# One attention unit's query path moves from plain projections with TensorE transpositions to split projections with VectorE transpositions, under a new order of the program

## The chip, the cores and the metric

The kernel runs on one core of a Trainium2 chip. Its time is the device time of one execution in microseconds (us). Five engines work side by side, each through its own queue in program order: TensorE (PE, with its weight loads as PEld), VectorE (DVE), ScalarE (ACT), GpSimd (POOL) and SyncE (SP), which issues all the transfers. An instruction starts when its engine is free and the semaphores that it waits on have come.

## The reference: what is computed

A linear attention over 8 batches of 8 heads (576 tokens, 64 wide, 128 random features), whose output is the input of one feed-forward block with a softmax gate and a layer norm over 4608 tokens.

```python
def phi(x):
    proj = np.einsum('bhsd,df->bhsf', x, w_phi)
    proj = proj - np.max(np.abs(proj), axis=-1, keepdims=True)
    return np.concatenate([np.exp(proj), np.exp(-proj)], axis=-1)
q_p, k_p = (phi(q), phi(k))
kv = np.einsum('bhsf,bhsd->bhfd', k_p, v)
num = np.einsum('bhsf,bhfd->bhsd', q_p, kv)      # den: the same with z, the sum of k_p
...
h = x @ w_in                                      # x: num / den, 4608 x 512
e = np.exp(h - h_max); sm = e / e.sum(); solu = h * sm
ln = (solu - mu) / np.sqrt(var + 1e-06) * g_ln
out = ln @ w_out
```

## The kernel before, in words

The attention is cut into 16 units (two per batch, four heads each), and a unit into two halves of two heads ("sub" 0 and 1). A unit's keys are projected in three groups of token tiles (4, 1 and 4 tiles: `k_rows`, line 557, and `by_block`, line 551, into PSUM tiles `pjk`); VectorE takes the row maximum (`m<-pjk`) and subtracts it (`ek<-pjk,m`); ScalarE makes the two exponentials. `visit` (line 594) then sums keys times values on TensorE (`kv`), 80 records of the trace, and from the fifth half on it first runs the previous half's queries against their finished sums (`num`, 72 records).

The queries have two paths, chosen by the tuple `Q_PLAIN` (line 30).

The **plain** path (units in `Q_PLAIN`; lines 612 to 651) goes as the keys do: float32 projections with tokens on the partitions (`pjq`), a maximum (`m<-pjq`) and a subtraction (`dq<-pjq,m`) on VectorE per group and head, then 24 transpositions on TensorE (`dT<-ident,dq`), and ScalarE's exponentials straight out of PSUM (`fq<-dT`).

The **split** path (all other units; lines 653 to 710) splits the queries into a high part (ScalarE, `hq`) and a remainder (GpSimd, `lq`), and projects them in three products with features on the partitions (`pq`). The maximum lies across partitions there. So VectorE transposes blocks of 32 by 32 (`blk<-pq`), reduces (`m<-blk`) and combines the quarters in seven small instructions (the rest of `q_max`, line 681); GpSimd subtracts (`blk<-blk,m`, `q_sub`, line 696); VectorE transposes back (`fq<-blk`, `q_back`, line 702); ScalarE makes the exponentials from SBUF (`fq<-fq`).

The feed-forward block runs in 18 groups of two token tiles. A group's input comes back through HBM (`xT<-dx`), GpSimd and ScalarE make sums and high and low parts (`S`, `ah`, `al`), and TensorE forms seven products of six matmuls each (`U` four times, `h` three times: `product`, line 978). VectorE joins them in PSUM (`moe_keep`, line 993; `moe_join`, line 1012, a custom instruction `h<-h,c` or `h<-U,c`). Softmax, layer norm, a turn of the tile through HBM and 24 matmuls `o` per tile follow. The first product can't start before the input weights are prepared: eight loads of 64 bit numbers (`wraw`) are made into float32 by two VectorE instructions each, `w<-wraw` (`w_low_bits`, line 394) and `w<-whi,w` or `w<-wraw,w` (`w_join_bits`, line 400), and split on ScalarE and GpSimd (`wb_l`, `wt_l`; four of the eight make the output weights, which are needed at the first `o`).

All of this is a list of some 2600 operations (`plan.op`). Nothing is scheduled when the kernel is built: `SEQUENCE` (lines 55 to 192) is the whole program order as a list of operation numbers, and `Plan.order` (line 243) only walks it and hands each tile its buffer. Each engine's queue is this list with the other engines left out. PSUM has six one-bank tiles for everything (`PSUM_BUFS`, line 45), handed out in the list's order. Every instruction has line 274 in the trace, the helper that keeps program order, so it is found by its tiles.

```python
Q_PLAIN = (0, 1, 2)
...
for u in range(2 * B):
    b, qd = u // 2, u % 2
    qsp = u not in Q_PLAIN
```

Of the kernel before, what the change touches and what calls it, by code (L numbers as in the profile page):

```python
# [29 lines left out]
Q_PLAIN = (0, 1, 2)  # L30
# [255 lines left out]
def linear_attention_then_moe(ctx: ExitStack, tc, qT, qT2, kT, v, w_phi, w_in, g_ln, w_out, out):  # L286
# [490 lines left out]
    def features(n):  # L777
        u, sub = n // 2, n % 2
        return [(u, "qe", sub, c, *x) for c in range(2) for x in (((0,), (1,)) if u not in Q_PLAIN else QP)]

    QP = [(j, s) for j in range(2) for s in range(2)]
# [3 lines that stand above are left out]
        st = states[u] = {"u": u, "b": b, "qd": qd}  # L785
# [532 lines left out]
```

## Time and profile before

| | us |
|---|---|
| median of 3 runs | 640.41 (637.32 to 641.12) |
| the profiled execution | 634.97 |
| its span, first to last instruction | 633.2 |
| PE busy in the span | 617.8 |
| DVE, ACT, POOL busy | 475.3, 458.1, 432.0 |

The profiled execution is the one that the trace shows; it lies below the three runs. Its span is 1.77 us shorter than its time. Times within the trace count from the span's first instruction. PE's busy share counts overlapping matmuls once, and a matmul that is stretched by a late operand still counts as busy.

### The profile page before, as it was taken

The numbers are of one execution on the slowest core, as the hardware profiler recorded it, in microseconds if no ns is written. First come the engines' busy times: TensorE is split into PE (matmuls) and PEld (weight loads), VectorE is DVE, ScalarE is ACT, GpSimd is POOL, SyncE is SP. The second block draws the span as 40 slices with busy tenths as digits, with TensorE's granted clock in tenths as the row PEclk, the third lists the DMA queues.
The fourth block names the chain that finished last, engine by engine and source line by source line (L and its number), as shares of the span: only waits on it lengthen the run. The fifth ranks groups of instructions, "written<-read, shape, count | busy, mean of one in ns | idle before, by whom it ended". The sixth has DMA issues, their size and how long they took to land.

```text
span 633.2 us, 19010 instructions
## 1 busy us (share of the span) xinstructions
PE 617.8 (98%) x7558; PEld 525.0 (83%) x7558; DVE 475.3 (75%) x995; ACT 458.1 (72%) x842; POOL 432.0 (68%) x468
## 2 busy tenths in 40 slices
PE   6999899999999999999999999999999999999997
PEld 5988688878888888888888888888888888888887
DVE  6999999787868885877876779988897973453540
ACT  4999798677957877477877667887776686466743
POOL 0568998777658864856786586657876675487732
PEclk9999999999999999999999999999999999999999
DMA  8886354754438374455574627545535355356441
GB/s 282 310 274 206 95 162 165 217 144 158 133 115 228 118 218 146 132 143 129 155 229 158 166 87 227 161 126 194 157 128 145 103 165 182 82 158 182 150 134 67
DMA packets 100200, 103.38 MB, mean 163 GB/s; under 512 B 50448, under 2 KB 73232, under 8 KB 99600
## 3 DMA queue, kind: packets, MB, share of 16 engines
q1 hardware_dynamic: 100112, 102.18, 52.8%
q8 instruction: 59, 0.97, 0.6%
q14 instruction: 29, 0.24, 0.1%
HBM read 64.92 MB, written 37.22 MB: 161 GB/s over the span
## 4 chain that ended last, share of the span: by engine, by line
PE 88%; DVE 6%; ACT 2%; DMA 2%; issue 1%; SPq 0%; ACTq 0%; DVEq 0%
PE o L274 31%; PE U L274 15%; PE h L274 12%; PE num L274 10%; PE kv L274 9%; PE pjk L274 5%; PE pq L274 4%; DVE m L274 2%; DVE w L274 1%; DVE ek L274 1%; PE pjq L274 1%; DVE dq L274 1%; DMA xT<-dx 1%; ACT fq L274 1%; DMA out<-os 1%
## 5 line engine op out<-in xcount | busy, mean ns | idle before, releaser
L274 PE MATMUL o<-w_out_h,uhs 128*128 128x512 f32 x280 | 112.4, 402 | 0.0
L274 POOL TENSOR_TENSOR uls<-uTs,uhs 128x1024 fp32r<-128x1024 f32 x35 | 83.7, 2390 | 41.9 <-ACT uhs L274 28.9
L274 PE MATMUL o<-w_out_l,uhs 128*128 128x512 f32 x280 | 109.4, 391 | 0.0
L274 PE MATMUL o<-w_out_h,uls 128*128 128x512 f32 x280 | 109.2, 390 | 0.0
L274 ACT ACTIVATE ek<-ek 128x512 f32<-128x512 f32 (+1 forms) x160 | 90.6, 584 | 16.9 <-DVE ek L274 16.1
L274 PEld LDWEIGHTS num<-kvf,fq 128*64 128x64 f32 x2304 | 70.0, 138 | 9.6 <-issue 5.0
L274 PE MATMUL kv<-rv,ek 128*64 128x65 f32 x2048 | 76.9, 222 | 0.0
L274 PE MATMUL num<-kvf,fq 128*64 128x65 f32 x2304 | 74.4, 223 | 0.1
L274 POOL TENSOR_TENSOR blk<-blk,m 128x1152 f32<-128x1152 f32 x26 | 55.6, 2138 | 27.3 <-DVE m L274 27.3
L274 ACT ACTIVATE fq<-fq 128x640 f32<-128x640 f32 (+1 forms) x104 | 69.4, 679 | 6.1 <-DVE fq L274 5.6
L274 PEld LDWEIGHTS kv<-rv,ek 128*64 128x64 f32 x2048 | 71.0, 138 | 0.8 <-ACT fq L274 0.2
L274 ACT ACTIVATE eu<-h,nm 128x1024 f32<-128x1024 f32 x36 | 40.1, 1115 | 36.4 <-DVE nm L274 31.7
L274 PEld LDWEIGHTS o<-w_out_h,uhs 128*128 128x128 f32 x280 | 52.6, 188 | 12.5 <-issue 0.2
L274 POOL TENSOR_TENSOR al<-S,ah 128x512 fp32r<-128x512 f32 x36 | 47.5, 1320 | 21.8 <-ACT ah L274 20.9
L274 PEld LDWEIGHTS o<-w_out_h,uls 128*128 128x128 f32 x280 | 52.6, 188 | 11.2
L274 PEld LDWEIGHTS o<-w_out_l,uhs 128*128 128x128 f32 x280 | 52.6, 188 | 10.3
L274 POOL TENSOR_TENSOR y<-E,rc 128x512 f32<-128x512 f32 x64 | 43.6, 704 | 21.3 <-DVE rc L274 19.1
L274 DVE TENSOR_REDUCE m<-pjk 128x4 f32<-128x512 f32 (+1 forms) x80 | 48.9, 620 | 11.4 <-PE pjk L274 11.1
L274 DVE SCALAR_TENSOR_TENSOR eu<-h,eu 128x1024 f32<-128x1024 f32 x36 | 43.8, 1218 | 18.1 <-ACT eu L274 17.7
L274 DVE STREAM_TRANSPOSE ub<-eu 128x1024 f32<-128x1024 f32 x35 | 43.1, 1233 | 14.3 <-ACT eu L274 5.5
L274 DVE STREAM_TRANSPOSE blk<-pq 128x320 f32<-128x320 f32 (+1 forms) x104 | 43.4, 455 | 10.8 <-PE pq L274 10.7
L274 POOL TENSOR_TENSOR lq<-rawq,hq 128x576 fp32r<-128x576 f32 x26 | 37.2, 1432 | 20.9 <-ACT hq L274 20.1
(113 smaller groups left out, 1558.4 us busy)
## 6 DMA issues: line engine op xcount, KB each, us to landing
du<-ub SPq DMA_DIRECT2D x35, 512.0 KB, 3.0
uTs<-du SPq DMA_DIRECT2D x140, 128.0 KB, 3.2
dx<-y SPq DMA_DIRECT2D x32, 288.0 KB, 2.7
out<-os SPq DMA_DIRECT2D x35, 256.0 KB, 3.0
rv<-in_v SPq DMA_DIRECT2D x32, 264.0 KB, 4.1
rawk<-in_k SPq DMA_DIRECT2D x32, 256.0 KB, 4.0
xT<-dx SPq DMA_DIRECT2D x64, 128.0 KB, 3.3
rawq<-in_q SPq DMA_DIRECT2D x26, 288.0 KB, 3.9
```

The lines of the kernel that those rows point to most:

```text
L274: return self.tc.keep_in_program_order(method(*args, **kwargs))
```

## The change

Unit 2 (the first unit of batch 1) leaves `Q_PLAIN`, so that its queries take the split path, as those of units 3 to 15 do. The operations are numbered anew, and `SEQUENCE` is another list: not the old one with unit 2's rows replaced, but one whose first rows already differ (keys ahead of queries at the start). No function changes.

```diff
-Q_PLAIN = (0, 1, 2)
+Q_PLAIN = (0, 1)
...
 SEQUENCE = (
-    120, 3, 121, 4, 76, 110, 124, 87, 177, 78, 20, 95, 0, 122, 88, 200, 77, 125, 96, 111, 79, 89, 83, 80, 81,
...
+    76, 3, 4, 78, 79, 83, 80, 110, 111, 81, 0, 112, 87, 84, 85, 90, 120, 113, 86, 91, 116, 117, 126, 114, 77,
...
```

Two places show what the list does. The first is VectorE's queue in the stretch in which unit 2's queries are handled, between the turn of unit 1's output (`y<-y`) and the last weight pieces. Before, with `m<-pjq` and `dq<-pjq,m` as unit 2's maximum and subtraction and `blk<-pq` as a transposition of unit 3:

```order
L274 TENSOR_TENSOR ek<-pjk,m 128x4x128
L274 TENSOR_REDUCE m<-pjq 128x2
L274 TENSOR_TENSOR dq<-pjq,m 128x256
L274 TENSOR_REDUCE m<-pjk 128x4 x2
L274 TENSOR_TENSOR ek<-pjk,m 128x4x128
L274 STREAM_TRANSPOSE blk<-pq 128x320 x2
L274 TENSOR_REDUCE m<-pjq 128x4
L274 TENSOR_TENSOR dq<-pjq,m 128x512
L274 TENSOR_REDUCE m<-pjq 128x4
L274 TENSOR_TENSOR dq<-pjq,m 128x512
L274 TENSOR_SCALAR w_5_1255<-wraw_909 128x1024
L274 TENSOR_SCALAR w_7_1257<-wraw_1054 128x1024
```

After the change the same stretch holds unit 2's transpositions, reduction and the small instructions that combine quarters (`m_1067` is unit 2's maximum, first half):

```order
L274 TENSOR_TENSOR ek<-pjk,m 128x4x128
L274 STREAM_TRANSPOSE blk<-pq 128x320 x2
L274 RECIPROCAL rc<-rc 128x18
L274 STREAM_TRANSPOSE blk<-pq 128x256 x2
L274 TENSOR_REDUCE m_1067<-blk 128x36
L274 COPY m4p<-m_1067 64x36
L274 TENSOR_TENSOR m_1067<-m_1067,m4p 64x36
L274 COPY m4p<-m_1067 32x36
L274 TENSOR_TENSOR m_1067<-m_1067,m4p 32x36 x4
L274 STREAM_TRANSPOSE y<-y 128x576
L274 TENSOR_REDUCE m<-pjk 128x4
L274 STREAM_TRANSPOSE blk<-pq 128x320 x2
```

So VectorE has more instructions of other kinds here, and the remaining weight pieces move behind them. The second place is TensorE's queue from unit 2's first visit to its second. Before, with unit 2's transpositions (`dT`) and plain projections (`pjq`) around a part of unit 3's split projection (`pq`):

```order
L274 MATMUL kv<-vz_70,ek 64x65 x2
L274 MATMUL dT<-ident,dq 128x128 x6
L274 MATMUL pjq<-wph,rawq_1038 128x256
L274 MATMUL pjk<-wph,rawk 128x128 x8
L274 MATMUL dT<-ident,dq 128x128 x6
L274 MATMUL pq<-hq,w_hh 128x320 x2
L274 MATMUL pq<-hq,w_ll 128x320 x2
L274 MATMUL pq<-lq,w_hh 128x320 x2
L274 MATMUL pjq<-wph,rawq_1019 128x128 x8
L274 MATMUL num<-kvf,fq 64x65 x36
```

After, from the same last rows of the visit on, with unit 2's split projections ahead of and behind a key projection:

```order
L274 MATMUL kv<-vz_70,ek 64x65 x2
L274 MATMUL pq<-hq,w_hh 128x320 x2
L274 MATMUL pq<-hq,w_ll 128x320 x2
L274 MATMUL pq<-lq,w_hh 128x320 x2
L274 MATMUL pq<-hq,w_hh 128x256 x2
L274 MATMUL pq<-hq,w_ll 128x256 x2
L274 MATMUL pq<-lq,w_hh 128x256 x2
L274 MATMUL pjk<-wph,rawk 128x128 x8
L274 MATMUL pq<-hq,w_hh 128x320 x2
L274 MATMUL pq<-hq,w_ll 128x320 x2
L274 MATMUL pq<-lq,w_hh 128x320 x2
L274 MATMUL pq<-hq,w_hh 128x256 x2
```

The transpositions `dT` of unit 2, which before stood between and behind the first feed-forward products too, are gone from TensorE's queue, and with them changes between float32 and split (fp32r) matmuls. From the last of the first group's seven products on (`h` with the weights `wt_h`, six matmuls) both queues hold the same set of matmuls.

## Rows read from the trace of the kernel before

**Rows 1.** The page's line on the busy time of each engine (share of the span, number of instructions).

```profile
PE 617.8 (98%) x7558; PEld 525.0 (83%) x7558; DVE 475.3 (75%) x995; ACT 458.1 (72%) x842; POOL 432.0 (68%) x468
```

**Rows 2.** Busy time by stretch: the stretch in us, its length, busy us and number of instructions of PE, PEld, DVE, ACT and POOL, granted clock, DMA share, GB/s.

```profile
5.96:68.40 62.44, 56.18 (x1125) 49.11 (x1125) 59.27 (x93) 53.11 (x116) 39.34 (x28) 1.00 0.79 267
...
83.38:629.99 546.61, 544.51 (x6211) 461.43 (x6208) 402.40 (x877) 390.06 (x697) 376.50 (x421) 1.00 0.52 155
629.99:633.20 3.21, 0.00 (x0) 0.00 (x0) 0.00 (x0) 0.47 (x1) 0.00 (x0) 1.00 0.12 41
```

**Rows 3.** What VectorE waited for between 5.96 and 83.38 us: instruction, who released it, us in total, times, longest. Of the first row's 7.0 us, 5.96 lie ahead of VectorE's first instruction.

```profile
DVE m L274 <- PE pjq L274: 7.0, 3, 6.0
DVE m L274 <- PE pjk L274: 1.0, 3, 0.5
DVE h L274 <- PE h L274: 0.6, 1, 0.6
...
DVE rc L274 <- ACT rc L274: 0.3, 1, 0.3
DVE y L274 <- POOL y L274: 0.2, 1, 0.2
```

**Rows 4.** TensorE in order of time: start, us, instruction, merged count. The first product `U`, and the last product of the first group, which stands right behind unit 3's first visit.

```profile
68.40 0.47 PE L274 MATMUL U<-wb_h,ah 128*128 128x512 f32 x1 [2.15 <-DVE blk L274]
...
83.38 0.50 PE L274 MATMUL h<-wt_h,ah 128*128 128x512 f32 x1
```

**Rows 5.** VectorE in order of time, the same columns: a pair of short transpositions, a combination of quarters from its reduction to its successor, the joining instruction that the last product waits for, and the transposition back of one half with its successor.

```profile
67.81 0.77 DVE L274 STREAM_TRANSPOSE blk<-pq 128x256 f32<-128x256 f32 x2
...
72.41 1.34 DVE L274 TENSOR_REDUCE m<-blk 128x36 f32<-128x1152 f32 x1
...
75.17 0.67 DVE L274 TENSOR_TENSOR c<-U,c 128x512 f32<-128x512 f32 x1
...
81.48 0.70 DVE L274 CUSTOM_DVE_ANT_0 h<-U,c 128x512 f32<-128x512 f32 x1
...
85.82 1.55 DVE L274 STREAM_TRANSPOSE fq<-blk 128x320 f32<-128x320 f32 x4
87.29 1.22 DVE L274 SCALAR_TENSOR_TENSOR eu<-h,eu 128x1024 f32<-128x1024 f32 x1
```

**Rows 6.** VectorE in order of time early on: plain maxima and subtractions one behind the other, wide (512 elements) and narrow (256); and a pair of the long transpositions.

```profile
11.01 0.68 DVE L274 TENSOR_REDUCE m<-pjq 128x4 f32<-128x512 f32 x1
11.61 0.41 DVE L274 TENSOR_REDUCE m<-pjk 128x2 f32<-128x256 f32 x1
11.94 0.68 DVE L274 TENSOR_TENSOR dq<-pjq,m 128x512 f32<-128x512 f32 x1
...
58.59 0.91 DVE L274 STREAM_TRANSPOSE blk<-pq 128x320 f32<-128x320 f32 x2
```

**Rows 7.** TensorE in order of time: a plain projection of one group, nine transpositions behind it and their successor; the narrow projection and its successor; the longer of a half's two split projections and its successor.

```profile
18.30 1.16 PE L274 MATMUL pjq<-wph,rawq 64*128 64x128 f32 x16
19.39 1.20 PE L274 MATMUL dT<-ident,dq 128*128 128x128 f32 x9
20.52 0.28 PE L274 MATMUL kv<-rv,ek 128*64 128x65 f32 x2
...
54.26 0.60 PE L274 MATMUL pjq<-wph,rawq 128*128 128x256 f32 x2
54.79 0.47 PE L274 MATMUL pjk<-wph,rawk 64*128 64x128 f32 x2
...
158.57 0.41 PE L274 MATMUL pq<-hq,w_hh 64*128 64x320 f32 x2
...
159.12 1.05 PE L274 MATMUL pjk<-wph,rawk 64*128 64x128 f32 x16
```

**Rows 8.** The chain that ended last, in order of time (start, us, what): a product behind float32 matmuls and the product behind that one.

```profile
83.45 1.58 PE h L274 x6
85.03 1.36 PE U L274 x6
```

**Rows 9.** The costliest groups of ScalarE and GpSimd on both query paths: instruction and count, busy us and mean ns of one, idle time before it.

```profile
L274 ACT ACTIVATE fq<-fq 128x640 f32<-128x640 f32 (+1 forms) x104 | 69.4, 679 | 6.1 <-DVE fq L274 5.6
L274 ACT ACTIVATE fq<-dT 128x320 f32<-128x320 f32 (+1 forms) x48 | 17.5, 421 | 0.2
L274 ACT CAST hq<-rawq 128x576 fp32r<-128x576 f32 x26 | 17.3, 668 | 2.3 <-PE pq L274 2.3
...
L274 POOL TENSOR_TENSOR blk<-blk,m 128x1152 f32<-128x1152 f32 x26 | 55.6, 2138 | 27.3 <-DVE m L274 27.3
L274 POOL TENSOR_TENSOR lq<-rawq,hq 128x576 fp32r<-128x576 f32 x26 | 37.2, 1432 | 20.9 <-ACT hq L274 20.1 <-ACT os L274 0.8
```

**Rows 10.** GpSimd between 22.09 and 83.38 us: busy us of the 61.29, and what it waited for (the 20.2 us end at 22.09).

```profile
22.09:83.38 61.29, 54.25 (x39) 1.00 0.60 188
...
POOL wb_l L274 <- DVE w L274: 20.2, 1, 20.2
POOL y L274 <- DVE rc L274: 5.3, 3, 2.0
```

**Rows 11.** The eight low-bit instructions of the weights: their busy us, mean ns and idle time before; and from another view the shortest, median and longest in ns.

```profile
L274 DVE TENSOR_SCALAR w<-wraw 128x1024 uint32<-128x1024 uint32 x8 | 9.3, 1174 | 0.0
...
L274 DVE TENSOR_SCALAR w<-wraw x8: 682/1254/1739, 17.5 to 64.5; 128x1024 uint32<-128x1024 uint32 x8
```

270 rows, old and new, of the table SEQUENCE are left out of this document.

## The prediction

> **What bounds the kernel now.** The page's busy line comes first: PE 617.8 of 633.2 us, every other engine under 480 [rows 1]. Read by itself it says that TensorE sets the time. So the second view asks where that holds. By stretch, from 83.38 us to TensorE's last matmul at 629.99 it is busy 544.5 of 546.6 us, and DVE only 402 [rows 2]. There TensorE is the bound, and less work for it, or an earlier start, is time won. From 5.96 to 68.40 us it is otherwise: DVE is busy 59.3 of 62.4 us, PE 56.2, ACT 53.1, POOL 39.3 [rows 2]. PE's 56.2 contain matmuls that were stretched by late operands, since busy time counts these too. VectorE is the tight engine of this head, and TensorE follows the PSUM tiles that it frees: the first `U` came after 2.15 us of idle time that ended with a VectorE transposition [rows 4].
>
> The two stretches meet at a place that I use as the joint of the whole sum: the last of the first group's products, `h` with the weights `wt_h`, which starts at 83.38 us [rows 4]. The order of both kernels has the same set of matmuls from there on. It needs VectorE's join `h<-U,c`, which ended at 81.48 + 0.70 = 82.18 [rows 5], and the end of unit 3's first visit, which stands right ahead of it on TensorE and used up the 1.2 us between. So the end of the kernel is this start, plus 546.6 us, plus 3.2 us behind the last matmul [rows 2], plus 1.8 us around the span: 83.4 + 546.6 + 3.2 + 1.8 = 635.0, the profiled execution. What moves this start moves the end.
>
> **The change, part by part.** All of unit 2's query work lies ahead of the joint in both orders.
>
> *TensorE loses.* Plain: a projection of one group takes 19.39 - 18.30 = 1.09 us, twice; the narrow one 54.79 - 54.26, about 0.5; nine transpositions 20.52 - 19.39 = 1.13, so 24 take 3.0. Sum 5.7. Split: the longer of a half's two projections takes 159.12 - 158.57 = 0.55, so four take 2.2 at most [rows 7]. TensorE saves 3.5 us, all of it in the head.
>
> *VectorE gains work.* Plain: wide instructions start 0.60 apart (11.01 to 11.61), narrow ones 0.33 [rows 6]; eight wide and two narrow are 5.5 us. Split, per half: two long transpositions 0.83 (0.91 less the overlap of 0.08 that wide pairs show), two short ones 0.69 (0.77 less the same), the maximum with its small instructions 2.76 (72.41 to 75.17), four transpositions back 1.47 (85.82 to 87.29) [rows 5, 6]. That is 5.8, for two halves 11.5. VectorE gets 6.0 us more. By the new order, two more instructions (a wide key subtraction, 0.6, and a reciprocal of 18 numbers per row, for which I take 0.2, the mean of the maximum's seven small instructions, (2.76 - 1.34) / 7) stand ahead of the joining `h<-U,c`, and nothing else is added or taken: 6.8 us more ahead of the joint.
>
> *ScalarE* comes out nearly even: 17.5 / 3 = 5.8 us of exponentials for a plain unit against 69.4 / 13 = 5.3 and two casts of 0.67 for a split one, 0.9 more [rows 9]. It had 9 us free in the head [rows 2], which hides it; without that cover it would cost its 0.9. *GpSimd* gets two remainders and two subtractions, 2 x (1.43 + 2.14) = 7.1 us [rows 9]. From 22.09 to 83.38 it was busy 54.3 of 61.3 us [rows 10], so 7.0 us were free: the work just fits, if the idle gaps can be filled. Of them 5.3 us were spent waiting for VectorE's reciprocals, and the new order puts unit 2's remainder ahead of such a wait. I count nothing here, and keep the overflow for a rival. Loads stay at about the same bytes.
>
> *The sum at the joint.* Before, VectorE went from 5.96 to 82.18, 76.2 us, of which it waited 1.04 + 1.0 + 0.6 + 0.3 + 0.2 = 3.1 [rows 3, 5]; 73.1 were work. After: 79.9 of work, from the same start, since the same two loads stand ahead of the first projection. The waits w are the unknown. Under 0.2 I don't go: that is the one old wait that has to do with neither a projection nor ScalarE. And 3.1 is what the old order had, with less work to hide waits behind. The old ones for `pjq` (1.0) largely belonged to unit 2 and go; a new one is likely where unit 2's transposition back follows GpSimd's subtraction. I take 2.0. The join then ends at 5.96 + 79.9 + 2.0 = 87.9 and the product starts there, not at 83.38: 4.5 us later. With w from 0.2 to 3.1 it is 2.7 to 5.6 later. The 3.5 us that TensorE saves lie in front of this wait, and buy nothing.
>
> *Behind the joint* the matmuls are the same but stand with fewer changes between float32 and split kinds: 50 changes into split ones where there were 54. A product behind such a change takes 1.58 us, the next 1.36 [rows 8], so four save 0.9. Sum: 4.5 - 0.9 = 3.6 us later; from 1.8 (w = 0.2) to 5.6 (w = 3.1, nothing saved). On the profiled execution that is 634.97 + 3.6 = 638.6. The runs' median lies 5.4 us above the profiled one, so I add the difference to the median: 640.41 + 3.6 = 644.0.
>
> **Rivals.**
>
> *TensorE decides everywhere.* If VectorE has hidden room in the head, the joint moves forward by what TensorE saves: -3.5 - 0.9 = -4.4, 636.0. For it: 98% [rows 1]. Against it: 3.1 us of idle DVE can't take 6.8 us of work. It decides if the join ends ahead of 82.2. The Trainium skill, "Perfetto Trace Analysis", "Identifying the Most-Contended Engine", has one optimize the engine with the highest occupancy first, which is this rival's time; the same page warns, for TensorE, that matmul occupancy is no good measure, and adds that the engine can change between regimes, and the trace agrees with that: DVE leads up to 68 us.
>
> *It all comes out even.* VectorE's waits shrink to 0.2, and TensorE's 2.1 us of idle time behind the joint (546.6 - 544.5, [rows 2]) are filled as well: 2.7 - 0.9 - 2.1 = -0.3, 640.1. For it, a queue that is nearly always behind waits little. Against it, two things must go right together.
>
> *GpSimd's extra work stretches VectorE's weight pieces.* The eight `w<-wraw` take from 0.68 to 1.74 us for one shape [rows 11], the first of them at 17.5, when GpSimd had not yet begun its weight work [rows 10]. With GpSimd's free 7.0 us gone, all eight may take 1.74: 8 x (1.74 - 1.17) = 4.6 us more in the head (1.17 is their mean now). With GpSimd late as well, this puts the joint at 3.6 + 4.6 = 8.2 us later, 648.6; half of it gives 646.3. It decides if five or more of the eight grow long. The Trainium skill, "SBUF — State Buffer", "Who interferes with whom", says that VectorE in its two-port modes and GpSimd exclude each other for a whole instruction; the spread of one shape agrees, and by that rule a fuller GpSimd costs VectorE time, as this rival has it.
>
> **How the numbers follow.** The forecast (642 to 646) gets 0.56, TensorE everywhere 0.10, even 0.14, the stretched head (646 to 650) 0.20. Leaving out the first rival and the far end of the last, the range is 638.0 to 650.0. About 1% is what a measurement of this kernel can tell from no change. Faster by that (under 634.0) needs the first rival and 2 us more: 0.04. Slower by it (over 646.8) is most of the last rival and the forecast's upper edge: 0.21. Within: 0.75.
>
> **What would show it.** Right: the last product of the first group starts near 88 us, behind a VectorE row `h<-U,c` that ended just before, with idle TensorE ahead of it; DVE busy near 95% from 6 to 85 us; from that product to the last matmul 545 to 547 us at granted clock 1.00; DVE's total up by 6 us, POOL's by 7. Wrong: that product ahead of 83 us (TensorE or ScalarE set the head), or a stretch behind it that is longer than 548 us (a later wait took over, or the clock fell), or `w<-wraw` above 11 us in sum with the joint past 90 us.

## The result, and the profile after

| | kernel before | changed kernel |
|---|---|---|
| median (runs) | 638.57 us (19) | 641.93 us (19) |
| lowest to highest | 635.74 to 641.12 | 639.52 to 643.78 |
| profiled execution, its span | 634.97, 633.2 | 641.06, 639.3 |
| start of the last product of the first group ("the joint") | 83.38 | 90.50 |
| mean granted TensorE clock of the profiled execution | 1.000 | 0.992 |

The ratio is 1.0064, with a 95% interval of 1.0048 to 1.0079: 4.1 us slower, within 1% (the two medians stand 3.4 us apart). The forecast was 3.6 us. Its absolute 644.0 stands 2 us above the measured median because it was added to the median of the first three runs, 640.41, and the later runs of the kernel before were lower. The two profiled executions differ by 6.1 us, more than the medians: that of before was faster than all its 19 timed runs.

The page's busy line of the changed kernel answers to [rows 1]:

```profile
PE 617.8 (97%) x7524; PEld 523.7 (82%) x7524; DVE 482.6 (75%) x1017; ACT 459.7 (72%) x836; POOL 439.1 (69%) x472
```

VectorE is up by 7.3 us and GpSimd by 7.1. TensorE has 34 instructions less and the same busy time. One reason shows in its clock. Busy time by stretch (PE, PEld, DVE, ACT, POOL, then granted clock, DMA share, GB/s), as in [rows 2], and a finer cut of TensorE alone (busy, granted clock, DMA share, GB/s):

```profile
5.96:70.38 64.42, 56.86 (x1097) 49.14 (x1095) 61.66 (x102) 53.91 (x112) 42.62 (x31) 0.92 0.80 262
70.38:90.50 20.12, 15.29 (x208) 11.88 (x205) 18.86 (x41) 14.75 (x27) 20.00 (x16) 1.00 0.20 41
90.50:636.10 545.60, 543.44 (x6208) 460.51 (x6208) 402.08 (x876) 388.67 (x695) 375.29 (x419) 1.00 0.51 155
```

```profile
52.00:57.00 5.00, 3.54 (x32) 0.98 0.45 140
57.00:67.00 10.00, 6.36 (x60) 0.50 0.81 249
67.00:70.00 3.00, 3.00 (x109) 1.00 1.14 228
```

The reader is to see three things. Behind the joint the kernel is as it was: 639.3 - 90.50 = 548.8 us to the end of the span, against 549.8. Between the first `U` and the joint TensorE has 4.8 us of idle time in 20.1, and GpSimd 0.1. In the kernel before GpSimd was as full in this stretch, but TensorE had no idle time:

```profile
68.40:83.38 14.98, 14.98 (x211) 12.64 (x211) 13.63 (x27) 12.61 (x26) 14.92 (x12) 1.00 0.21 57
```

And TensorE ran at half its clock (0.50, the level of 1.2 GHz) from 57 to 67 us, after it had been busy for 3.54 of 5.00 us. The kernel before had no such stretch in its profile. In these 10 us VectorE was busy for 9.63 us and GpSimd throughout, and behind them TensorE waited for GpSimd, so the rows of this profile don't show that the halved clock held up the joint.

TensorE in order of time (answers to [rows 4]): its first `U`, waits for GpSimd's `lq` and `al`, and the joint, whose releaser `nm` is the minimum that VectorE reads out right behind the join `h<-U,c`.

```profile
59.04 0.64 PE L274 MATMUL pq<-lq,w_hh 64*128 64x320 f32 x2 [2.22 <-POOL lq L274]
...
70.38 0.50 PE L274 MATMUL U<-wb_h,ah 128*128 128x512 f32 x1
71.90 0.50 PE L274 MATMUL U<-wb_h,al 128*128 128x512 f32 x1 [0.79 <-POOL al L274]
...
76.66 0.50 PE L274 MATMUL U<-wt_h,al 128*128 128x512 f32 x1 [1.72 <-POOL al L274]
...
81.92 0.50 PE L274 MATMUL h<-wb_h,al 128*128 128x512 f32 x1 [0.94 <-POOL al L274]
...
90.50 0.50 PE L274 MATMUL h<-wt_h,ah 128*128 128x512 f32 x1 [1.14 <-DVE nm L274]
```

Before, TensorE's one long wait here was for VectorE [rows 4]; now the long ones are for GpSimd's `lq` and `al`. VectorE's rows show the group's first join, the join of the forecast, and its weight pieces by line (count, busy us, mean ns, idle before):

```profile
83.26 0.70 DVE L274 CUSTOM_DVE_ANT_0 h<-h,c 128x512 f32<-128x512 f32 x1 [0.66 <-PE h L274]
...
89.70 0.69 DVE L274 CUSTOM_DVE_ANT_0 h<-U,c 128x512 f32<-128x512 f32 x1
```

```profile
L274 DVE TENSOR_SCALAR w<-wraw 128x1024 uint32<-128x1024 uint32 x8 | 9.2, 1152 | 0.3 <-DMA wraw<-in_w_in 0.3
L274 DVE SCALAR_TENSOR_TENSOR w<-wraw,w 128x1024 uint32<-128x1024 uint32 x4 | 9.1, 2275 | 0.0
```

The join ended at 90.39, not at 87.9. VectorE waited 2.8 us in sum from 5.96 on, so 81.6 us were work. The first join, `h<-h,c`, stands 7.2 us ahead of the joint here and in all eight runs below that have this order, so what moves the joint among them is the start of this row. It waited 0.66 us for TensorE's product `h`, which had waited 0.94 us for GpSimd's `al`: VectorE's path and GpSimd's arrive within a microsecond of each other. (The last join writes the second token tile's `h`, for which `PSUM_BUFS` has a buffer of its own, one, beside the six one-bank tiles, so it has to wait for the first tile's softmax.) The low-bit instructions took in sum what they did before (9.3, [rows 11]); the four joins that read SBUF on both sides took 2.28 us in the mean. GpSimd by stretch (busy, then as above) answers to [rows 10], where its idle time was counted as one sum of 7.0 us:

```profile
22.09:50.58 28.49, 22.04 (x17) 1.00 0.74 253
50.58:90.50 39.92, 38.97 (x29) 0.87 0.47 121
```

It is free for 6.5 us early and for 1.0 us from 50.6 us on, where most of unit 2's work falls. Cut at the same time, the kernel before had 5.1 of its 7.0 us early and 1.9 late:

```profile
22.09:50.58 28.49, 23.38 (x19) 1.00 0.78 260
50.58:83.38 32.80, 30.87 (x20) 1.00 0.44 125
```

### The profile page after: what moved, and what is told of

It is laid out like the page before. It is cut to its first block, busy times and chain, and to the rows that moved or that the text cites. A ratio compares the mean times of both kernels' runs of the same rounds, so it can differ in the third digit from the quotient of the medians.

```text
span 639.3 us, 18940 instructions
## 1 busy us (share of the span) xinstructions
PE 617.8 (97%) x7524; PEld 523.7 (82%) x7524; DVE 482.6 (75%) x1017; ACT 459.7 (72%) x836; POOL 439.1 (69%) x472
## 4 chain that ended last, share of the span: by engine, by line
PE 88%; DVE 5%; DMA 2%; ACT 2%; POOL 1%; issue 1%; SPq 0%; DVEq 0%; POOLq 0%; ACTq 0%
PE o L274 31%; PE U L274 15%; PE h L274 12%; PE num L274 10%; PE kv L274 10%; PE pjk L274 6%; PE pq L274 4%; DVE w L274 2%; DMA wraw<-in_w_in 1%; DVE m L274 1%; PE pjq L274 0%; DVE ek L274 0%; ACT w L274 0%; DMA wph<-in_w_phi 0%; DVE c L274 0%
## 5 line engine op out<-in xcount | busy, mean ns | idle before, releaser
L274 PEld LDWEIGHTS num<-kvf,fq 128*64 128x64 f32 x2304 | 71.3, 139 | 10.3 <-issue 5.8
L274 ACT ACTIVATE fq<-fq 128x640 f32<-128x640 f32 (+1 forms) x112 | 75.0, 679 | 6.4 <-DVE fq L274 5.7
L274 POOL TENSOR_TENSOR blk<-blk,m 128x1152 f32<-128x1152 f32 x28 | 60.2, 2151 | 23.9 <-DVE m L274 23.3
L274 PE MATMUL num<-kvf,fq 128*64 128x65 f32 x2304 | 75.9, 224 | 0.6 <-issue 0.2
L274 DVE STREAM_TRANSPOSE blk<-pq 128x256 f32<-128x256 f32 (+1 forms) x112 | 47.2, 453 | 17.8 <-PE pq L274 17.8
L274 ACT ACTIVATE eu<-eu,ms 128x1024 f32<-128x1024 f32 x36 | 41.4, 1149 | 18.7 <-DVE eu L274 18.5
L274 PE MATMUL pjk<-wph,rawk 64*128 64x128 f32 (+1 forms) x544 | 47.7, 293 | 4.6 <-DMA wph<-in_w_phi 3.9
```

The source lines that it names most:

```text
L274: return self.tc.keep_in_program_order(method(*args, **kwargs))
```

## The experiments

The measured results together; the joint and the clock are those of each profiled execution, the ratio is to the kernel before on the same chip (637.1 to 637.7 us there, 638.57 beside the changed kernel). The expectations give absolute times that start from 638.6 and 641.9; what follows compares ratios.

| run | median us | ratio, 95% interval | joint us | clock |
|---|---|---|---|---|
| changed kernel | 641.93 | 1.0064 [1.0048, 1.0079] | 90.50 | 0.992 |
| e2_after_less_vector | 642.45 | 1.0084 [1.0063, 1.0104] | 90.95 | 0.989 |
| e6_after_less_gpsimd | 639.72 | 1.0033 [1.0012, 1.0054] | 88.70 | 0.989 |
| e11_after_less_both | 638.93 | 1.0017 [0.9996, 1.0039] | 88.08 | 0.992 |
| e13_after_less_both_two_y | 637.61 | 1.0008 [0.9987, 1.0029] | 86.01 | 0.995 |
| e12_after_two_y | 640.93 | 1.0054 [1.0037, 1.0072] | 90.45 | 0.991 |
| e4_after_pieces_psum | 640.81 | 1.0056 [1.0036, 1.0076] | 89.52 | 0.989 |
| e14_after_two_y_pieces | 640.75 | 1.0049 [1.0031, 1.0067] | 88.19 | 0.989 |
| e7_after_fill_tensor | 642.40 | 1.0073 [1.0052, 1.0094] | 90.08 | 0.992 |
| e3_before_more_vector | 645.04 | 1.0133 [1.0106, 1.0159] | 95.11 | 0.989 |
| e5_before_pieces_psum | 635.26 | 0.9965 [0.9940, 0.9990] | 83.33 | 0.997 |
| e9_new_order_behind | 638.82 | 1.0030 [1.0007, 1.0054] | 83.14 | 0.997 |
| e8_path_alone | 653.76 | 1.0270 [1.0231, 1.0308] | 100.04 | 0.981 |

The theory at the start was the prediction's: VectorE's added work ahead of the joint sets the time. The first rival was GpSimd, the second TensorE's halved clock, the third the order.

**Less work for VectorE in the changed kernel (e2_after_less_vector).**

```diff
+        if st["u"] == 2:
+            nc.vector.memset(m, 2.0)
+            return
         nc.vector.tensor_reduce(
```

> The changed kernel, with VectorE's chain for the maximum of unit 2 (two reductions over 128x1152 of 1.32 us and seven small instructions behind each, 2 x 2.6 = 5.2 us by the profile after) replaced by two memsets to 2.0: unit 2's maximum of q is left out. GpSimd's subtraction, the transpositions and TensorE's products stay as they are. If VectorE's work ahead of the joint decides, the time falls by 4 to 5.2 us from the changed kernel's 641.9: 636.7 to 638 us, as fast as the kernel before or faster. If GpSimd (full from 56 to 90 us) or its hold on VectorE's weight pieces decides, the removed instructions only become a wait: 640.5 to 642. If TensorE's halved clock from 57 to 67 us is what was lost, also 640 or more.

It came no earlier. What became of the 5.2 us is in VectorE's waits from 50 to 91 us (instruction, who released it, us in total, times, longest):

```profile
DVE fq L274 <- POOL blk L274: 3.7, 2, 3.2
DVE h L274 <- PE h L274: 2.6, 1, 2.6
DVE y L274 <- POOL y L274: 1.6, 1, 1.6
```

Two of the three are GpSimd itself. The third is TensorE, and its row shows who held it:

```profile
74.00 0.50 PE L274 MATMUL U<-wb_h,al 128*128 128x512 f32 x1 [2.53 <-POOL al L274]
...
75.44 0.63 PE L274 MATMUL h<-wb_l,ah 128*128 128x512 f32 x1
```

The last row shows that a part of this wait is TensorE's own. Behind its 2.53 us of idle time the granted clock fell a second time, to 0.51 from 75 to 78 us, where a matmul of this shape took 0.63 us in place of 0.39. From the row at 74.00 to VectorE's first join it took 9.7 us; the same products took 8.1 in the profile of the run with both engines relieved and two buffers for `y`. So the removed work turned into waiting, most of it for GpSimd and some 1.6 us of it for the clock, and the theory in its simple form falls for the changed kernel.

**More work for VectorE in the kernel before (e3_before_more_vector).**

```diff
         max_of(st, "mq", "pjq", g, j)
+        if st["u"] == 2:
+            n = 2 if j is None else 4
+            for _ in range(2):
+                row_max(st["mq", g, j][:, :n], tokens(st["pjq", g][j], n))
```

> The kernel before, with each of the five maxima of unit 2's plain path taken three times in place of once: ten more reductions on VectorE, eight of 0.66 and two of 0.37 us, 6.0 us of work ahead of the joint, and nothing else. If VectorE's work ahead of the joint decides, the time rises by 5 to 6 us from 638.6: 643.5 to 644.6 us. If TensorE decides there, by 0 to 1: 638.6 to 639.6.

6.0 us of work cost 7.3 us by the medians, 8.5 by the ratio, more than the 5 to 6 expected. In the old head VectorE does decide, as the prediction read it, and the excess suggests that lateness there brings more with it: TensorE's granted clock fell in this profile too (0.989 in the mean, 1.000 in that of before). This profiled execution is the slowest of the six.

**Less work for GpSimd, and for both (e6_after_less_gpsimd, e11_after_less_both).** The first edit is below; the second run adds that of the run with less on VectorE.

```diff
-        hi_lo_sub(nc.gpsimd, st["lq", sub], st["rq", sub], st["hq", sub])
+        if st["u"] != 2:
+            hi_lo_sub(nc.gpsimd, st["lq", sub], st["rq", sub], st["hq", sub])
...
+        if st["u"] == 2:
+            return
         nc.gpsimd.tensor_tensor(
             out=blk, in0=blk, in1=st["m4", sub].unsqueeze(2).to_broadcast([P, NM, 32]), op=ALU.subtract
```

> The changed kernel, with what the change adds on GpSimd left out: unit 2's two remainders lq (TensorE's third product reads hq again, so its work stays) and the two subtractions of the maximum, 2 x 1.42 + 2 x 2.2 = 7.2 us. VectorE, ScalarE and TensorE keep all their work. The run before it, with 5.2 us less on VectorE, came no earlier to the joint (90.95 against 90.50), and its chain ran over GpSimd, which was busy without a break from 51 to 90 us. If GpSimd alone decides ahead of the joint in the changed kernel: 5 to 7 us faster than its 641.9, 635 to 637. If GpSimd and VectorE arrive together (the theory now): 1 to 2 us faster, because VectorE's weight pieces shrink a little beside a free GpSimd and then VectorE decides: 640 to 641. If VectorE alone decides, as predicted, also 640 to 642, but then the run with less on both gains no more than the 5.2 of VectorE lets expect. If TensorE's clock decides: 641 to 642.5.

> The changed kernel with both left out: unit 2's chain of the maximum on VectorE (5.2 us) and unit 2's remainders and subtractions on GpSimd (7.2 us). If GpSimd and VectorE arrive at the joint together, each alone gains little and both gain 4 to 6 us: 636 to 638, the joint at 84 to 87 us. If TensorE's halved clock between 57 and 70 us decides (0.50 there in the profile after and in the run with less on VectorE alone), it stays at 641 or above, since TensorE's work is the same and it waits more, not less. If TensorE's work in itself decides: 640 or above with a clock of 1.00.

With GpSimd relieved alone the time falls by some 2 us by the ratio. VectorE is then as tight as ever (2.8 us of waits up to the joint), and what it gained is in its weight pieces, by line:

```profile
L274 DVE TENSOR_SCALAR w<-wraw 128x1024 uint32<-128x1024 uint32 x8 | 10.7, 1340 | 0.0
L274 DVE SCALAR_TENSOR_TENSOR w<-wraw,w 128x1024 uint32<-128x1024 uint32 x4 | 5.8, 1452 | 0.0
```

16.5 us in place of 9.2 + 9.1 = 18.3: 1.8 less, and the joint is 1.8 earlier. One join shows what GpSimd has to do with it: in the changed kernel it ran beside the remainder `wt_l`, in this run while GpSimd stood idle (it waited 3.36 us for a load, up to 67.81).

```profile
65.26 3.40 DVE L274 SCALAR_TENSOR_TENSOR w<-wraw,w 128x1024 uint32<-128x1024 uint32 x1
62.41 5.16 POOL L274 TENSOR_TENSOR wt_l<-w,wt_h 128x1024 fp32r<-128x1024 f32 x2
```

```profile
65.75 1.20 DVE L274 SCALAR_TENSOR_TENSOR w<-wraw,w 128x1024 uint32<-128x1024 uint32 x1
```

But the run with less on VectorE has 16.7 us for these pieces with GpSimd's work unchanged, so what counts is beside what a piece falls, and not only how much GpSimd has to do.

With both relieved, 12 us of work gone, the time falls by 3.0 us by the ratio. That is less than the 4 to 6 expected, but the interval takes in no difference from the kernel before. GpSimd's 7.2 us bought 2.0 us alone and 4.3 on top of VectorE's; VectorE's 5.2 bought nothing alone and 1.0 on top of GpSimd's. Each of these is uncertain by some 2 us; together they point to GpSimd as the tighter of the two. In the run with both GpSimd waits for a transfer and VectorE for TensorE:

```profile
52.51 1.33 POOL L274 TENSOR_TENSOR y<-E,rc 128x512 f32<-128x512 f32 x2 [5.02 <-DMA dx<-y]
```

```profile
80.84 0.70 DVE L274 CUSTOM_DVE_ANT_0 h<-h,c 128x512 f32<-128x512 f32 x1 [5.08 <-PE h L274]
```

That names a candidate for a third chain: a half unit's output `y` has one buffer, which its transfer `dx<-y` must let go before the next `y`; the fourth `dx` allows the loads `xT` of the first group. SyncE's queue in order of time, of the kernel before and of the changed one, shows the fourth `dx` issued 4.0 us later:

```profile
42.99 0.33 SPq L274 DMA_DIRECT2D dx<-y  x1
...
48.76 0.33 SPq L274 DMA_DIRECT2D dx<-y  x1
...
55.54 0.33 SPq L274 DMA_DIRECT2D dx<-y  x1
```

```profile
45.55 0.33 SPq L274 DMA_DIRECT2D dx<-y  x1
...
53.83 0.33 SPq L274 DMA_DIRECT2D dx<-y  x1
...
59.57 0.33 SPq L274 DMA_DIRECT2D dx<-y  x1
```

**Two buffers for y (e12_after_two_y, e14_after_two_y_pieces, e13_after_less_both_two_y).** The buffer alone, then with two weight pieces in PSUM, then with both engines relieved.

```diff
-    y=1, m2k=2, S=2, A=4, A1=2, c=3, big=6, nm=4, sm=3, ms=2, mv=2, sa=2, sc=3,
+    y=2, m2k=2, S=2, A=4, A1=2, c=3, big=6, nm=4, sm=3, ms=2, mv=2, sa=2, sc=3,
```

> The changed kernel with two SBUF buffers in place of one for y, the output of a half unit on its way to DRAM. In the profile after, the products y of units 0 and 1 on GpSimd wait 1.9 and 0.8 us for the transfer dx<-y of the half unit before to let go of the buffer (2.6, 4.2 and 5.0 us in the runs with less on VectorE, with pieces in PSUM and with less on both), the second of these transfers takes 5 to 7 us to land beside two loads of q and a weight piece of 1 MB, and the fourth is issued at 59.6 us against 55.5 before: 4 us later, as much as the whole change costs. If this chain (y, dx, xT, S, al, U, h) is one of three that arrive at the joint together, the fourth dx comes 2 to 3 us earlier and the time falls by 1 to 2.5: 639.5 to 641 us. If it alone decides, 638 to 639. If VectorE alone decides, as predicted, 641.4 to 642.4.

> The changed kernel with two buffers for y and the pieces 4 and 6 in PSUM; the latter alone gave a ratio of 1.0056 to the kernel before, against 1.0064 of the changed kernel, though it takes 2 us from VectorE. With three chains together the two edits give more than their sum: 638 to 639.5 us. With VectorE alone, as much as the pieces alone: 640.5 to 641.2.

> The changed kernel with unit 2's chain of the maximum on VectorE and unit 2's remainders and subtractions on GpSimd left out, and with two buffers for y. The run with both left out and one buffer gave 638.9 us, with 5.0 us of wait of y for its buffer ahead of the third transfer. If that wait was what the 12 us of removed work turned into: 2 to 4 us less, 635 to 637, as fast as the kernel before or faster, with a joint at 84 to 86 us. If TensorE and its clock set the rest: 638 to 639.5.

Alone it gave nothing that its interval tells from the changed kernel, where 1 to 2.5 us were expected. The wait of `y` for the transfer is gone, but the fourth `dx` went out at the same time, because VectorE came to its transposition no earlier:

```profile
59.52 0.33 SPq L274 DMA_DIRECT2D dx<-y  x1
```

With the pieces in PSUM the joint of the profile was 2.3 us earlier, but its span 0.7 us longer, and the ratio fell by 0.0015: no more than the two edits alone give in sum, where more was expected. With both engines relieved the fourth `dx` goes out at 56.81 us, the joint is at 86.01, and the time is that of the kernel before within 0.3%; but against the run with one buffer the ratio fell by 0.0009 only, well inside the intervals, where 2 to 4 us were expected. So the times show two bounds, VectorE and GpSimd, and that relieving both brings the time back within the noise. They don't show a third: the way of `y` is seen in the rows alone, as waits once the other two are relieved. What is left in this run, a joint 2.6 us later than in the kernel before, is seen there too:

```profile
65.79 2.89 POOL L274 TENSOR_TENSOR S<-xT 128x256 f32<-128x256 f32 x2 [3.78 <-DMA xT<-dx]
...
69.34 1.26 POOL L274 TENSOR_TENSOR al<-xT,ah 128x512 fp32r<-128x512 f32 x1
```

```profile
70.65 0.50 PE L274 MATMUL U<-wb_h,al 128*128 128x512 f32 x1 [1.17 <-POOL al L274]
```

```profile
78.77 0.70 DVE L274 CUSTOM_DVE_ANT_0 h<-h,c 128x512 f32<-128x512 f32 x1 [5.63 <-PE h L274]
```

GpSimd waits for the first load `xT`, forms three sums `S` and only then the first `al`; TensorE waits for this `al`, and VectorE for TensorE. In the kernel before the first `S` began at 64.10 and, behind it alone, the first `al` at 65.09. The granted clock was 0.50 again at 60 to 66 us, but TensorE's 1.17 us of waiting lie behind that, so it didn't hold up the joint of this profile.

**The weight pieces in PSUM (e4_after_pieces_psum, e5_before_pieces_psum).**

```diff
-BY_PSUM = (0, 1, 2, 3)
+BY_PSUM = (0, 1, 2, 3, 4, 6)
```

In the kernel before the added pieces are 4 and 7.

> The changed kernel, with the high part of the weight pieces 4 and 6 in a PSUM bank in place of SBUF, as the pieces 0 to 3 have it: VectorE's joins of these two read PSUM. In the profile after, the four joins that read SBUF on both sides took 2.28 us in the mean (1.23 to 3.40), the four that read PSUM 1.21. If the longer ones are stretched by what GpSimd does beside them, the two joins fall to 1.2 us each and the joint comes up to 2.2 us earlier: 639.7 to 640.8 us. If the stretched joins don't matter to the end, or a join from SBUF takes its 1.2 to 3.4 us for a reason of its own that a wait replaces, 641.5 to 642.5. If the one PSUM bank that is taken makes the pieces wait for one another, slower than 642.5.

> The kernel before, with the high part of the weight pieces 4 and 7 in PSUM. With the changed kernel the same edit (pieces 4 and 6) gave 640.81 against 641.9. If VectorE's work ahead of the joint decides in the kernel before (three more reductions of each maximum made it 7.3 us slower for 6.0 us of work), the joins shrink from 1.9 us in the mean to 1.2 and the time falls by 0.7 to 1.5 us: 636.2 to 637.1 beside the 637.7 of the kernel before on this chip. If not, within 0.5 us of it.

In the changed kernel the ratio fell by 0.0008 only, well inside the intervals, although all weight pieces together took 20.5 us of VectorE where they had taken 23.2. In the kernel before they took 18.0 in place of 21.8, and it ran faster by 1.8 us by the medians and 2.2 by the ratio, a little more than expected: the fastest version here, ahead of both kernels. Its rows of the joins, from PSUM and from SBUF:

```profile
L274 DVE SCALAR_TENSOR_TENSOR w<-whi,w 128x1024 uint32<-128x1024 uint32 x6 | 7.2, 1208 | 0.7 <-ACT whi L274 0.5
L274 DVE SCALAR_TENSOR_TENSOR w<-wraw,w 128x1024 uint32<-128x1024 uint32 x2 | 3.0, 1498 | 0.0
```

By these values the same relief of VectorE pays in the old head and hardly in the new one, which fits the pair of runs at the top; but the two gains, 0.0035 and 0.0008, are each uncertain by some 0.0025, so that they differ is not shown.

**Keeping TensorE busy (e7_after_fill_tensor).**

```diff
+        for _ in range(4 if st["u"] == 2 else 0):
+            for j, r in enumerate(HEADS):
+                nc.tensor.matmul(pq[j][:, :n], lhsT=w_hh[r, :], rhs=hq[r, cs], start=True, stop=True)
         for i, (w, x) in enumerate(((w_hh, hq), (w_ll, hq), (w_hh, lq))):
```

> The changed kernel, with four more pairs of matmuls ahead of each of unit 2's four groups of q's split products; the next product starts its sum anew and drops them. In the profile after, TensorE's granted clock was 0.50 from 58 to 66 us, where TensorE had been busy for 1.4 to 1.8 us of every 2 before; the kernel before had no such fall. The added matmuls fill TensorE there. If the halved clock costs time at the end, it stays at 1.00 and the time falls by 1 to 2 us: 640 to 641. If VectorE decides and TensorE has room there, the clock stays up and the time is unchanged within 0.5 us: 641.4 to 642.4. If TensorE has no room ahead of the joint, the added 8 to 10 us of matmuls make it slower: 643 or more.

TensorE by stretch, as above:

```profile
57.00:62.00 5.00, 1.69 (x19) 0.95 0.78 268
62.00:67.00 5.00, 4.84 (x59) 0.50 0.87 219
67.00:70.00 3.00, 3.00 (x87) 0.78 1.13 227
```

The clock held for some 5 us longer and then fell all the same. The time did not change. Length times what is missing to 1.00 gives 3.4 us here and 5.1 in the changed kernel's rows (an estimate): the run takes away about a third of the fall and shows no gain, but it doesn't hold the clock up, so from the times what the clock costs stays open.

**The order behind the joint, and the path in the old order (e9_new_order_behind, e8_path_alone).** The first is `SEQUENCE` of the kernel before for its first 420 operations and of the changed kernel for the rest, with `Q_PLAIN = (0, 1, 2)`. The second has `Q_PLAIN = (0, 1)` and the old order with unit 2's new operations put in. In both the table is 13 lines longer, so the helper stands at L287.

> The kernel before with its own path and its own order up to the joint (the first 420 operations of its table), and behind it the remaining operations in the order of the changed kernel. In the profiles the stretch from the joint to the end is 549.8 us before and 548.8 after, which the prediction put down to four switches less between float32 and split products. If that 1.0 us comes with the order behind the joint, this kernel is 0.5 to 1 us faster than the kernel before: 636.7 to 637.2 beside 637.7. If the new order behind the joint is itself what costs the changed kernel, 3 to 4 us slower: 641 to 642. If neither, within 0.5 us.

> Unit 2 on the split path, in the order of the kernel before: each operation that both have stays at its place (some 140 places ahead and 34 moved by a few because of a buffer), unit 2's new ones stand behind the neighbours on their engine that they have in the changed kernel. If the path costs and the new order only makes room for it, the time is that of the changed kernel or more: 642 to 647 us. If the new order is what costs, 638 to 640. If half and half, 640 to 642.

The first was 1.9 us slower than the kernel before (0.4 to 3.4 by its interval), none of the three expected sizes. Its profile shows where, behind the seam of the two orders:

```profile
92.31 0.80 PE L287 MATMUL h<-wb_h,ah 128*128 128x512 f32 x1 [2.96 <-DVE eu L287]
```

That wait is neither kernel's: the run says nothing clear on the order behind the joint. The second was 17 us slower than the kernel before, more than the 642 to 647 us expected. Its fourth `y` waited long and the joint came at 100 us:

```profile
60.79 1.32 POOL L287 TENSOR_TENSOR y<-E,rc 128x512 f32<-128x512 f32 x2 [5.97 <-DVE rc L287]
...
100.04 0.50 PE L287 MATMUL h<-wt_h,ah 128*128 128x512 f32 x1
```

In these old places the split path costs far more than in the new ones. That speaks against the new order as what costs the changed kernel its time; since mine is one arrangement among many, it doesn't show it.

## Why the prediction was right, and where it was not

*The head is VectorE's, the rest TensorE's.* Right for the kernel before: 6.0 us of added VectorE work cost 7 to 8.5 us. *What moves the joint moves the end.* Right for the profiled pair, in which the joint moved by 7.1 us and the span by 6.1. In all profiles together the stretch from the joint to the end of the span took from 548.7 to 552.9 us, so small moves of the joint can be lost behind it: with two buffers for `y` and the pieces in PSUM it came 2.3 us earlier and the end 0.7 us later. The other signs came as named: the join ended 0.1 us ahead of the joint, VectorE was busy for 80.5 of the 84.5 us up to it (95%), and from the joint to the last matmul it took 545.6 us at a clock of 1.00.

*TensorE's savings buy nothing.* Right: fewer instructions, and 4.8 us of idle time ahead of the joint. The rival in which TensorE decides everywhere, 636.0, is refuted, and so is the even one, 640.1: the changed kernel is slower by at least 0.48%.

*VectorE has 6.8 us more.* Mis-sized: its work to the join rose from 73.1 to 81.6 us, by 8.5. The joins of the weights (9.1 us for 7.7) and two small `w_ll` (1.6 for 0.6) more than cover the excess of 1.7. The rival of the stretched pieces named the wrong instructions: the `w<-wraw` that it watched stayed at 9.2 us in sum, the joins grew. That a working GpSimd has a part in it is shown by the join that took 3.40 us beside `wt_l` and 1.20 beside an idle GpSimd; that unit 2's added work there is what stretched the joins is not shown. By the Trainium skill, "SBUF — State Buffer", "Who interferes with whom", a VectorE instruction with two SBUF inputs contends with a GpSimd instruction that reads SBUF, and one with at most one SBUF input, outside the two-port modes, doesn't; the trace agrees in that the joins from PSUM took 1.20 to 1.22 us in the mean of each of these profiles, and those from SBUF 1.23 to 3.40 in that of the changed kernel.

*Waits of 2.0 us.* 2.8 in the profile, inside the 0.2 to 3.1.

*GpSimd: "I count nothing here".* This step failed. The 7.0 us of idle time were one sum over 61 us, but they lay early: from 50.6 us on the kernel before had 1.9 us free. There fall both of unit 2's subtractions and its second remainder, and the new order moves unit 3's first remainder there from 49.1 us: 7.5 us of work in all, of which the changed kernel has 1.0 us to spare. GpSimd became a bound beside VectorE. With VectorE's 5.2 us removed the time did not fall at all, with GpSimd's 7.2 removed it fell by 2.0. That the number came out all the same is in part luck. VectorE and GpSimd got about the same extra work (8.5 and 7.1 us), so that a sum made for one of them stood for the other as well; this is argued, no run shows it. And the profiled pair, on which the sum was built, misses it by more than the medians do: the joint came 7.1 us later where the sum had 4.5, and the time was 6.1 us longer where it had 3.6.

*The way of `y`.* Not in the prediction. The new order sends out the outputs of units 0 and 1 by 2.6 to 5.1 us later, and with both engines relieved GpSimd waits for them. That this costs time beside the other two is not shown.

*Behind the joint, 0.9 us less.* The profiled pair gives 1.0. This agrees in size and is not shown in its cause: in the other profiles with the changed kernel's order this stretch took from 548.7 to 551.8 us.

## What to carry to other kernels

Idle time of an engine is a cover only at the place where the new work lands: cut the sum by stretches before you count a cost at nothing. Where two engines are full at one place, relieving one proves nothing about it; relieve each alone and both together, and look at what the removed work turned into. An edit that pays in one order of the work (here two weight pieces in PSUM, 0.35%) has to be measured again in another, where a second engine may stand right behind the first (here 0.08%, a difference that the intervals don't settle). A run that takes work away can bring a new cost of its own, so its rows have to be read too: the relief of VectorE was hidden in part by a second fall of the clock.

## What the runs showed of the hardware

TensorE's granted clock fell to 0.50 for about 10 us in the head of the changed kernel, where TensorE waited for GpSimd and VectorE, and came back during a stretch in which it was busy throughout. Each of the 19 runs of the changed kernel shows a mean of 0.987 to 0.995. The kernel before has a lower mean than 1.000 in some executions and not in others, and it goes with its time: 26 of its 75 runs that were measured beside the experiments have a mean of 0.999 or 1.000 and took 634.4 to 637.0 us (median 635.9), 25 have 0.995 or less and took 636.9 to 641.7 (median 639.1). So the spread of this kernel's times goes with the clock. At the same mean, 0.992, the two kernels stand closer than their medians: 639.8 us in 4 runs of the kernel before, 641.1 in 6 of the changed one. Whether the clock costs the time, or lateness costs both, the times don't tell apart. The rows show both cases: in the changed kernel's profile TensorE waited for GpSimd behind the fall, while in that of the run with less on VectorE a second fall lay on the path to the joint and took some 1.6 us.

A join of 128x1024 numbers took 3.40 us with both inputs in SBUF beside a working GpSimd, 1.20 with GpSimd idle, and 1.20 to 1.22 in the mean with one input in PSUM.
